# Eight matmuls of an attention kernel's opening moved into the projection, and a PSUM copy cut into two quarters

## The chip, the cores and the metric

The kernel runs on one core of a Trainium2 chip. The metric is the device time of one execution in microseconds (us). A run lists two numbers: its **time**, and its **span**, which is the time from the first to the last instruction in the records of that execution. The time is longer than the span, and I call the difference the time outside the span.

## The reference

```python
# B, Sq, D = 8, 32, 1024; Hq, Hkv, Sk, Dh = 32, 4, 8192, 128; all bfloat16
W = 2048                                    # the last W of the cache are used
q = (x @ wq).reshape(B, Sq, Hq, Dh).transpose(0, 2, 1, 3)
k = jnp.repeat(k_cache[:, :, Sk - W:, :], 8, axis=1)
v = jnp.repeat(v_cache[:, :, Sk - W:, :], 8, axis=1)
p = softmax(einsum("bhqd,bhkd->bhqk", q, k) * Dh ** -0.5)
o = einsum("bhqk,bhkd->bhqd", p, v)
return o.transpose(0, 2, 1, 3).reshape(B, Sq, Hq * Dh) @ wo
```

## The kernel before

There are 32 units (8 batches by 4 KV heads). A unit is four steps; each step multiplies four K tiles with the queries of eight heads (scores), takes the exponential on ScalarE, and multiplies the result with V two steps later. TensorE does the multiplications, and also the Q projection, the output projection, and the turning (transposing) of some K tiles. Its results lie in PSUM, from where VectorE or ScalarE copies them. The 256 rows of x are two row tiles of 128, and wq, the weight matrix of the Q projection, arrives in 8 chunks of 128 rows; the "late" matmuls make the second row tile of heads 4 to 7, which the first scores don't need. The opening, which the change edits, must make Q of the first KV head and a transposed K0 before the first scores:

```python
self.ps_m = pool("ps_m", 2, long_ctx, space=PSUM)
self.ps_s = pool("ps_s", 2, space=PSUM)       # scores, and in the opening K0's transposes
...
def start(self):
    ...
    wq0 = self.load_wq(0, 0, (1, 1, 1, 1)) + self.load_wq(0, 1, (2, 1, 1))  # chunks 0..3, then 4+5, 6, 7
    ...                                       # then K0, V0, K1, ... on the same queue
    x_turn(0, self.ps_m, "m"); x_turn(1, self.ps_s, "s_ps")
    ...
    for c in range(self.DC):                  # 8 chunks of D
        for h in range(self.rep):             # 8 heads: 4 with both row tiles, 4 with the first only
            q_mm(c, h)
        ...
    tp = [self.ps_s.tile([P, KT, P], BF16, name="kf_ps", tag="s_ps") for _ in range(2)]
    k_turn(0)                                 # 8 transposes: K0's first half
    q_copy(...)                               # Q of batch 0, out of PSUM (ScalarE, VectorE)
    k_copy(0)                                 # VectorE: the whole first half, 128x1024
    self.late = self.q_late(4, 2)             # second row tiles of heads 4 and 5
    self.late[0]()                            # head 4: 8 "late" matmuls
    k_turn(1)                                 # 8 transposes: K0's second half
    k_copy(1)
    self.va_copy(0)
    ...

# run(), every step:
    s_ps = self.ps_s.tile([P, CJ, UQ], FP32, name="s_ps")
    for jj in range(CJ):
        nc.tensor.matmul(s_ps[:, jj, :], lhsT=self.kT[ui][:, c * CJ + jj, :], rhs=q_u, start=True, stop=True)
```

The first scores take the buffer that held K0's first half, so they may only be written when that half has been copied out entirely.

## Time and profile before

| | before |
|---|---|
| time, median of 3 runs | 183.78 us (183.70 to 184.23) |
| span of the profiled run | 182.3 us |
| first transposes of x (x has landed) | 4.50 us |
| first transposes of K0 | 11.29 us |
| first scores | 12.69 us |
| start of the last long group of matmuls | 175.49 us |

The lines that the prediction reads (busy shares, the chain of waits, what TensorE's weight loads, PEld in the profile, stop for, VectorE's copies) are shown there. Two marks serve in all that follows. **S** is the start of the first scores in the timeline of TensorE. **E** is the start of the last group of 34 output matmuls in the chain of waits. Between S and E TensorE has the same instructions in both kernels:

```profile
12.69 0.61 PE L505 MATMUL s_ps<-QT,kT 128*128 128x256 bf16 x4
```

```profile
30.34 0.60 PE s_ps L505 x4
...
175.49 3.94 PE op_ps L322 x34
```

The first fence is a line of TensorE's timeline (start, duration, instruction), the second two of the chain of waits. E - S is 175.49 - 12.69 = 162.80 us.

### The profile page before, as it was taken

What the parts mean: (1) busy time and instruction counts of PE and PEld (TensorE: products, weight loads), DVE (VectorE), ACT (ScalarE), POOL (GpSimd) and SP (SyncE); (2) the same over time, 40 slices, a digit from 0 to 9 for tenths busy, and PEclk for the clock granted to TensorE, in tenths of its full rate; (3) what the DMA queues carried; (4) which work ended last, traced back from release to release, by engine and by line L of the source; (5) the groups of instructions that cost most, each with busy time, mean ns of one, the idle gap of its engine ahead of it and who ended that gap; (6) DMA issues with size and microseconds to landing.
All of it is one profiled execution on the core that took longest, in us unless ns stands there. A gap on an engine that the chain in (4) does not pass through costs nothing.

```text
span 182.3 us, 5017 instructions
## 1 busy us (share of the span) xinstructions
PE 177.4 (97%) x2026; PEld 152.0 (83%) x2041; DVE 126.0 (69%) x257; ACT 136.2 (75%) x147; POOL 89.2 (49%) x138
## 2 busy tenths in 40 slices
PE   7999999999999999999999999999999999999993
PEld 2899998998999999988787899988787788888853
DVE  0237799769887698487799565967587987554253
ACT  2228898896897888997878787887878788888800
POOL 2003564088770895936939707929606949600000
PEclk9999999999999999999999999999999999999999
DMA  6999999999999999999999999999999999980013
GB/s 169 395 400 408 225 388 350 233 296 260 377 391 244 322 257 365 374 295 313 304 378 377 391 269 271 369 245 365 258 318 273 331 289 344 218 167 0 0 41 85
DMA packets 52954, 51.73 MB, mean 284 GB/s; under 512 B 39744, under 2 KB 40256, under 8 KB 52928
## 3 DMA queue, kind: packets, MB, share of 16 engines
q1 hardware_dynamic: 52352, 50.90, 99.3%
q10 hardware_dynamic: 576, 0.49, 0.8%
q8 instruction: 16, 0.26, 0.6%
q14 instruction: 10, 0.08, 0.1%
HBM read 41.42 MB, written 0.52 MB: 230 GB/s over the span
## 4 chain that ended last, share of the span: by engine, by line
PE 91%; DMA 6%; SPq 1%; issue 1%; DVE 0%
PE o_ps L516 30%; PE s_ps L505 30%; PE op_ps L322 14%; PE q_ps L285 10%; DMA kT<-in_k_cache_dram 4%; PE q_ps L403 3%; DMA x_sb<-in_x_dram 2%; PE ql_ps L301 1%; PE tp L244 1%; SPq L208 1%; PE xT_ps L381 1%; PE kf_ps L395 0%; SPq L200 0%; DVE o_t L332 0%; PE cnt_ps L571 0%
## 5 line engine op out<-in xcount | busy, mean ns | idle before, releaser
L507 ACT ACTIVATE pT<-s_ps 128x1024 bf16<-128x1024 f32 x128 | 128.3, 1027 | 27.7 <-PE s_ps L505 27.4
L270 POOL TENSOR_SCALAR kTv<-kb 32x512 bf16<-32x512 bf16 x126 | 84.3, 669 | 51.3 <-DVE kb L259 32.1
L516 PE MATMUL o_ps<-va,pT 128*128 128x129 bf16 x1024 | 78.8, 220 | 0.1
L516 PEld LDWEIGHTS <-pT 128*128 128x128 bf16 x1024 | 68.5, 98 | 3.1
L505 PE MATMUL s_ps<-QT,kT 128*128 128x256 bf16 x336 | 50.4, 273 | 0.2
L505 PEld LDWEIGHTS <-kT 128*128 128x128 bf16 x336 | 31.7, 98 | 9.8 <-DMA kT<-in_k_cache_dram 0.4
L322 PE MATMUL op_ps<-wo_sb,OT 128*128 128x512 bf16 (+2 forms) x129 | 32.8, 353 | 0.6
L259 DVE STREAM_TRANSPOSE kb<-k_raw 128x512 bf16<-128x512 bf16 x44 | 29.7, 691 | 1.6 <-DMA k_raw<-in_k_cache_dram 1.2
L285 PE MATMUL q_ps<-xT,wq_sb 128*128 128x256 bf16 x192 | 28.3, 273 | 0.0
L438 DVE COPY va<-v_sb 128x2048 bf16<-128x2048 bf16 x30 | 25.4, 847 | 2.0 <-DMA v_sb<-in_v_cache_dram 1.6
L505 PE MATMUL s_ps<-QT,kTv 128*128 128x256 bf16 x176 | 26.4, 273 | 0.2
L268 DVE COPY kTv<-kb 32x512 bf16<-32x512 bf16 x50 | 23.1, 462 | 1.2
L444 DVE RECIPROCAL RL_all<-o_ps 128x2 f32<-128x2 f32 x32 | 5.3, 165 | 26.3 <-PE o_ps L516 26.1
L505 PEld LDWEIGHTS <-kTv 128*128 128x128 bf16 x176 | 16.9, 98 | 6.5 <-issue 0.4
L285 PEld LDWEIGHTS <-wq_sb 128*128 128x128 bf16 x192 | 16.9, 98 | 1.2
L450 DVE STREAM_TRANSPOSE OT<-o_sb 128x256 bf16<-128x256 bf16 x32 | 14.3, 445 | 1.1
L448 DVE TENSOR_TENSOR o_sb<-o_ps,RL_all 128x256 bf16<-128x256 f32 x32 | 13.6, 424 | 1.1
L322 PEld LDWEIGHTS <-OT 128*128 128x128 bf16 x144 | 11.4, 98 | 2.3 <-DVE OT L450 0.2
L436 POOL TENSOR_SCALAR va<-v_sb 128x2048 bf16<-128x2048 bf16 x2 | 3.8, 1897 | 17.0 <-DMA v_sb<-in_v_cache_dram 17.0
L288 ACT CAST QT<-q_ps 128x512 bf16<-128x512 f32 x12 | 7.0, 583 | 0.2 <-PE q_ps L285 0.2
L329 DVE TENSOR_TENSOR oacc<-op_ps,oacc 128x512 f32<-128x512 f32 x8 | 5.3, 662 | 2.0 <-PE op_ps L322 2.0
L332 DVE TENSOR_TENSOR o_t<-op_ps,oacc 128x512 bf16<-128x512 f32 (+2 forms) x6 | 3.1, 514 | 3.8 <-remote 2.2
(35 smaller groups left out, 45.0 us busy)
## 6 DMA issues: line engine op xcount, KB each, us to landing
v_sb<-in_v_cache_dram SPq DMA_DIRECT2D x30, 512.0 KB, 6.6
wo_sb<-in_wo_dram SPq DMA_DIRECT2D x16, 512.0 KB, 6.4
wq_sb<-in_wq_dram SPq DMA_DIRECT2D x13, 512.0 KB, 6.6
k_raw<-in_k_cache_dram SPq DMA_DIRECT2D x13, 512.0 KB, 5.7
wq_sb<-in_wq_dram SPq DMA_DIRECT2D x6, 256.0 KB, 4.5
v_sb<-in_v_cache_dram SPq DMA_DIRECT2D x4, 256.0 KB, 5.2
kT<-in_k_cache_dram SPq DMA_TRANSPOSE x36, 7.1
k_raw<-in_k_cache_dram SPq DMA_DIRECT2D x2, 256.0 KB, 5.7
```

The lines of the kernel that those rows point to most:

```text
L259: nc.vector.transpose(out=st["kb"][:, sl, :], in_=self.k_raw[ui][:, sl, :])
L268: nc.vector.tensor_copy(out=out, in_=in_)
L270: nc.gpsimd.tensor_scalar(out=out, in0=in_, scalar1=1.0, scalar2=1.0, op0=ALU.mult, op1=ALU.mult)
L285: nc.tensor.matmul(st[k][:, hl % 2, :], lhsT=self.wq_t[g, i][:, c % (DC // 2), hl * P:(hl + 1) * P], rhs=self.xT[:, c, :], start=(c == 0 a ...
L288: nc.scalar.copy(out=self.q_view(g)[:, :, 2 * k:2 * k + 2, :].rearrange("p b h s -> p h b s"), in_=st[k][:, :, :].rearrange("p h (b s) -> ...
L322: nc.tensor.matmul(ps[:, 0:w], lhsT=self.OT[:, gq, c, t * P:(t + 1) * P], rhs=self.wo_t[gq][:, c, n0:n0 + w], start=(k == 0), stop=(k == 7))
L438: self.nc.vector.tensor_copy(out=out, in_=in_)
L448: nc.vector.tensor_tensor(out=o_sb[:, :, :, :], in0=o_ps[:, :, 0:Dh].rearrange("p q (i c) -> p q c i", c=4), in1=rl[:, ui * QT_N:(ui + 1) ...
L450: nc.vector.transpose(out=self.OT[:, g * QT_N:(g + 1) * QT_N, :, b * self.Sq:(b + 1) * self.Sq], in_=o_sb[:, :, :, :])
L505: nc.tensor.matmul(s_ps[:, jj, :], lhsT=self.kT[ui][:, c * CJ + jj, :], rhs=q_u, start=True, stop=True)
L507: nc.scalar.activation(out=pT[:, :, :], in_=s_ps[:, :, :], func=ACT.Exp, bias=0.0, scale=self.scale)
L516: nc.tensor.matmul(o_ps[:, qt, 0:self.VW], lhsT=pT[:, jj, qt * P:(qt + 1) * P], rhs=va[:, j, 0:self.VW], start=(j == 0 and qt == 0), stop= ...
```

## The change

It means to give TensorE something to do where it stops for a chunk of wq, by putting head 4's late matmuls between the chunks, and to get the first K tiles out of PSUM sooner, by copying the first half in two quarters. The core of the diff:

```diff
-    def q_late(self, h0, n):
+    def q_late(self, h0, n, st=None):
...
-        def piece(i):
-            if i == 0:
+        def piece(i, cs=None):
+            if "ps" not in st:
                 st["ps"] = self.ps_m.tile([P, n, P], FP32, name="ql_ps", tag="m")
-            for c in range(DC):
+            for c in range(DC) if cs is None else cs:
...
-        def k_copy(half):
-            sl = slice(half * KT // 2, (half + 1) * KT // 2)
-            nc.vector.tensor_copy(out=self.kT[0][:, sl, :], in_=tp[half][:, 0:KT // 2, :])
+        def k_copy(copy, j0, j1):
+            copy(out=self.kT[0][:, j0:j1, :], in_=tp[2 * j0 // KT][:, j0 % (KT // 2):j0 % (KT // 2) + j1 - j0, :])
...
+        self.late = self.q_late(4, 2)
         for c in range(self.DC):
             for h in range(self.rep):
                 q_mm(c, h)
+            self.late[0](cs=(c,))
...
+        k_copy(nc.vector.tensor_copy, 0, KT // 4)
+        k_copy(nc.vector.tensor_copy, KT // 4, KT // 2)
         q_copy(nc.scalar.copy, 4, 8, 1, self.B // 2)
-        k_copy(0)
-        self.late = self.q_late(4, 2)
-        self.late[0]()
         k_turn(1)
-        k_copy(1)
+        k_copy(nc.vector.tensor_copy, KT // 2, KT)
```

More of the change, by code (lines that the diff above doesn't have):

```diff
@@ L291, in q_pieces @@
         return [lambda h=h, i=i: piece(h, i) for h0 in range(0, self.rep, n) for i in range(2) for h in range(h0, h0 + n)]
-    def q_late(self, h0, n):
+    def q_late(self, h0, n, st=None):
         nc, P, DC, B = self.nc, self.P, self.DC, self.B
-        st = {}
-        def piece(i):
-            if i == 0:
+        st = {} if st is None else st
+        def piece(i, cs=None):
+            if "ps" not in st:
                 st["ps"] = self.ps_m.tile([P, n, P], FP32, name="ql_ps", tag="m")
-            for c in range(DC):
+            for c in range(DC) if cs is None else cs:
                 nc.tensor.matmul(st["ps"][:, i, :], lhsT=self.wq_t[0, c // (DC // 2)][:, c % (DC // 2), (h0 + i) * P:(h0 + i + 1) * P],
@@ L306, in piece @@
                      in_=st["ps"][:, :, :].rearrange("p h (b s) -> p h b s", b=B // 2))
-        return [lambda i=i: piece(i) for i in range(n)]
+        return [lambda i=i, **kw: piece(i, **kw) for i in range(n)]
     def o_pieces(self, g, t, cuts=(512, 512), st=None):
```

## The prediction

> **What bounds the kernel now.** I read the page first, for the busy shares and for the chain of waits that ended last:
>
> ```profile
> PE 177.4 (97%) x2026; PEld 152.0 (83%) x2041; DVE 126.0 (69%) x257; ACT 136.2 (75%) x147; POOL 89.2 (49%) x138
> PE 91%; DMA 6%; SPq 1%; issue 1%; DVE 0%
> ```
>
> TensorE is the chain: 91% of the span, and no other engine has a lasting part in it. The 6% of DMA are two stretches, the load of x at the start and one transposing K load in the middle. So the next view was what TensorE's weight loads ever stop for (columns: engine, line, releaser, us in total, times, longest). I leave out the warm-up, which comes before any data:
>
> ```profile
> PEld L505 <- DMA kT<-in_k_cache_dram: 0.4, 1, 0.4
> PEld L505 <- issue: 0.4, 1, 0.4
> ...
> PEld L403 <- DMA wq_sb<-in_wq_dram: 0.2, 1, 0.2
> ```
>
> Three short stops between 5 and 170 us, all before 44 us. Their places decide this case. The timeline of weight loads puts the last of the three at 8.64 us (0.16 us, for a chunk of wq), the "issue" one at 30.31 us (the first K tile turned by VectorE and GpSimd, unit 4), and the DMA one at 43.46 us (second half of unit 6's K). Third view: the chain in order of time (start, us, what), through the part the change edits and around the last stop:
>
> ```profile
> 5.85 5.61 PE q_ps L403 x64
> 11.46 0.45 PE kf_ps L395 x8
> 11.90 0.45 PE ql_ps L301 x8
> 12.35 0.45 PE kf_ps L395 x8
> 12.80 0.50 PE s_ps L505 x4
> ...
> 34.05 0.45 PE s_ps L505 x4
> 34.50 0.66 SPq L200
> ...
> 36.74 6.67 DMA kT<-in_k_cache_dram
> 43.42 0.05 issue
> 43.46 0.61 PE s_ps L505 x4
> ```
>
> The second to fifth lines are the opening: eight transposes of K0's first half, the eight late matmuls of head 4, eight transposes of the second half, the first scores. The chain times an instruction by its end; the timeline gives starts of 11.29, 11.74, 12.19 and 12.69 us for the same four groups. The last fence shows that the path changes hands: up to 43.42 us a K transfer sets it, and only from there does TensorE run to the end without a stop.
>
> I don't believe the link at 34.05, from a score matmul to the issue of a K load. In the built program the loads issued from 10 to 37 us wait for TensorE only where it had passed long ago (the latest such count is unit 0's last scores, done at about 16.4 us); otherwise each waits for the load eight issues before it. A wait for several semaphores is easily put down to the wrong one. So 43.42 is a date of the DMA stream, and does not move when TensorE moves by tenths.
>
> The timeline of VectorE has the copies concerned (start, us, instruction):
>
> ```profile
> 11.94 0.69 DVE L399 COPY kT<-kf_ps 128x1024 bf16<-128x1024 bf16 x1 [0.45 <-PE kf_ps L395]
> 12.84 0.69 DVE L399 COPY kT<-kf_ps 128x1024 bf16<-128x1024 bf16 x1 [0.20 <-PE kf_ps L395]
> 13.44 0.68 DVE L438 COPY va<-v_sb 128x2048 bf16<-128x2048 bf16 x1
> ```
>
> A copy starts 0.65 us after the first of its eight transposes starts (11.29 to 11.94, 12.19 to 12.84), and a next copy may start about 0.09 us before the last one ends (13.53 against 13.44). The first scores start at 12.69, just after the first copy ends (11.94 + 0.69 = 12.63): the eight late matmuls filled that wait exactly.
>
> **What the Trainium skill says.** "TensorE: Matmul & The Clock Gate", section "Wait — 56ns, not 53.3ns?", gives 55.6 ns between matmuls with 128 columns; the trace has eight in 0.45 us, 56 ns, so it agrees. "VectorE: DVE Perf Modes", section "The TRN2 errata", has 120 cycles plus the elements over the mode's factor for a copy out of PSUM: at 0.96 GHz and a factor of two, 392 ns for 512 elements and 658 for 1024. The trace has 424 ns (the copy of xT, 128x512 bf16) and 691 ns: some 32 ns more, but the same slope, and a fixed part of about 157 ns which a split pays twice. I use the trace. "PSUM — Partial Sum Buffer", section "PSUM bank collisions raise a hardware error", asks for guarding by bank and quadrant, not by address. Half of K0 is 8 x 128 bf16 = 2 KiB a partition, which is one whole bank of those in that page, so neither a quarter's copy beside the other quarter's transposes nor a score write beside the second quarter's copy would be allowed. No run here shows a collision, but the waits in the program are laid out accordingly. "Perfetto Trace Analysis", section "What 'DMA-bound' means", names an issuing sequencer that is solid with DMA work as a bound of its own. The trace agrees in that SyncE's issues follow one another nearly without gaps from 17 to 43 us (single issues of 3.12, 4.67, 3.09 us).
>
> **The change part by part.** No instruction of TensorE is added or removed; eight matmuls move. VectorE gets one copy more.
>
> 1. The eight late matmuls (0.45 us) move into the projection, one after each chunk. The first needs a PSUM buffer whose last reader is ScalarE's copy of xT, over at about 6.42 us; it comes at 5.85 + 4 x 0.109 + 4 x 0.056 = 6.51, so no stop. By the fifth chunk four of them (0.22 us) have run, which is more than the 0.16 us stop for wq: it goes. The projection with its late matmuls ends 0.45 - 0.16 = 0.29 us later, so the transposes of K0 start at about 11.29 + 0.29 = 11.58 us.
> 2. The sixteen transposes now run on end: 11.58 to 12.48 us. In the old order TensorE reached this point at 12.64, so 0.16 us are gained to here.
> 3. The copies. In the built program the first quarter's copy waits for the count of the eighth transpose, not of the fourth, and the second has no wait of its own. So the first starts at 11.58 + 0.65 = 12.23; the second at 12.23 + 0.42 - 0.09 = 12.56, and it ends at 12.98.
> 4. The first scores' weight load waits for the count of both quarters. It has to: their PSUM buffer is the one both are copied from. So they start at 12.98 + 0.06 = 13.04 instead of 12.69: 0.35 us later. The gain of 0.16 becomes an idle stretch of 13.04 - 12.48 = 0.56 us, since the late matmuls that lay beside the copy are gone. The split itself costs 0.76 - 0.69 = 0.07 of it.
> 5. The second scores wait for the third copy, which starts at 12.98 - 0.09 = 12.89 and ends at 13.58. They come after four scores (0.44 us) and eight late matmuls (0.45 us), at 13.93: no stop. VectorE's later copies of the opening move by 0.05 us, so nothing waits for them that didn't.
> 6. So TensorE is 0.35 us behind from 13 us on. At 30.08 us it used to reach unit 4 and stood until 30.34, for VectorE's moves of K that ended at 30.20. That sequence starts at 19.23 us, when its K data land, and VectorE is then busy nearly throughout, so it doesn't move. TensorE now comes at 30.43: 0.26 of 0.35 us are absorbed, 0.09 stay.
> 7. At unit 6 TensorE used to be free at 42.73 + 0.44 = 43.17 and stood until 43.46, for the K data of 43.42. It now comes at 43.26 and starts at 43.46 as before. Nothing is left.
>
> The sum at the end is 0.35 - 0.26 - 0.09 = 0, against a median of 183.78 us. The opening has 0.55 us of slack (0.26 + 0.29) behind it, and the change moves it inside that slack. I add 0.05 us for what the slack may fail to take: 183.85 us.
>
> **The rivals.**
> - The opening's gain reaches the end. For it: 0.16 us of a stop goes, and the chain of waits runs through the opening. Against it: the wait for both quarters, and the two later stops, which would grow by any gain. It would make 183.6 us.
> - The loss reaches the end. For it: the chain draws the K load of 43.42 as released by TensorE at 34.05; if that is right, or if the moves of unit 4 follow TensorE, 0.09 to 0.35 us stay. Against it: the counts that the loads wait for. It would make 183.9 to 184.15 us.
> - The DMA stream shifts by itself. A landing at 19.23 or 43.42 that comes 0.3 us sooner or later moves the end by up to as much, in either kernel. The three runs before spread over 0.53 us, as much as all that is at stake.
> - A hidden wait, such as K0's second half landing later than the sixteen transposes now want it (at about 12.0 instead of 12.13 us). It would add tenths in the opening at most, and the slack takes them.
>
> **Range and chances.** The rivals span 183.6 to 184.15; runs differ by 0.3 us from the median and more. So 183.85, with 183.45 to 184.25 for 8 in 10. 2% are 3.7 us, ten times the largest single term, so within 2% is all but certain; a slower or faster state would be needed for anything else: 0.01 each.
>
> **What would show it.** Steps 1 and 2: no wait for wq in the projection, sixteen transposes on end from about 11.6 us. Steps 3 and 4: two copies of 0.42 us from about 12.2 us, the first scores at about 13.0, with TensorE's weight loads idle for some 0.5 us and VectorE's copy as releaser. Steps 6 and 7: the "issue" stop at unit 4 shrunk to nearly nothing, the first scores of unit 6's second half still at about 43.45, for the DMA. Wrong would be first scores before 12.7 us (then the quarters do overlap the transposes), or a landing at 43.42 that moves with TensorE, or a difference above 0.5 us.

## The result, and the profile after

| | before | changed |
|---|---|---|
| time, median | 183.74 us (183.55 to 184.23, 4 runs) | 184.80 us (184.65 to 185.08, 4 runs) |
| ratio of times | 1 | 1.0055 (95%: 1.0032 to 1.0079) |
| span of the profiled run | 182.3 us | 182.2 us |
| time less span, profiled run | 1.75 us | 2.88 us |

A ratio is the mean time of one kernel's fast runs over that of the other's in the same rounds, so it isn't quite the ratio of the medians. 184.80 us lies outside the predicted range of 183.45 to 184.25, and all four runs of the changed kernel are above it.

The profile after, page first (busy time by engine, chain by engine):

```profile
PE 177.9 (98%) x2041; PEld 152.2 (84%) x2041; DVE 125.5 (69%) x258; ACT 136.2 (75%) x147; POOL 89.1 (49%) x138
PE 93%; DMA 3%; SPq 1%; DVE 1%; issue 0%
```

VectorE has one instruction more. TensorE's 177.9 us against 177.4 is no change of work: the trace of before lacks 15 of 144 records of the output projection, hence 2026 matmuls against 2041 weight loads. In the chain, DVE has come in and DMA has halved. What weight loads stop for between 5 and 170 us (engine, line, releaser, us in total, times, longest):

```profile
PEld L402 <- DMA wq_sb<-in_wq_dram: 0.6, 1, 0.6
PEld L505 <- DVE kT L398: 0.6, 1, 0.6
```

Before, there were three stops, of 0.16 us in the projection, 0.36 us at unit 4 and 0.41 us at unit 6. Now there are two, both in the opening, and the two later ones are gone. (The weight load of K0's second transposes, for one, starts at 12.13 us and its matmuls at 12.19. So the two later stops cost the matmuls less than the whole 0.77 us: 0.57, by the comparison of E - S below.) The timeline shows where (weight loads, then TensorE's transposes, VectorE's copies, the first scores):

```profile
8.99 0.66 PEld L402 LDWEIGHTS <-wq_sb 128*128 128x128 bf16 x8 [0.60 <-DMA wq_sb<-in_wq_dram]
...
11.87 1.06 PE L395 MATMUL kf_ps<-ident,k_raw 128*128 128x128 bf16 x16
...
12.51 1.35 DVE L398 COPY kT<-kf_ps 128x512 bf16<-128x512 bf16 x3 [0.50 <-PE kf_ps L395]
...
13.33 0.61 PE L505 MATMUL s_ps<-QT,kT 128*128 128x256 bf16 x4 [0.41 <-DVE kT L398]
```

The first line is a stop of 0.60 us for the fifth chunk of wq, which the prediction held to be gone. The second: sixteen transposes on end. The third: three copies, no two of them apart, which start when the eighth transpose is done. The fourth: the first scores at 13.33 us, held up by the copies; before, they started at 12.69. The chain of the same run:

```profile
12.03 0.46 PE kf_ps L395 x8
...
12.51 0.77 DVE kT L398 x2
...
13.33 0.61 PE s_ps L505 x4
...
43.70 0.44 PE s_ps L505 x4
...
175.56 3.94 PE op_ps L322 x34
```

The chain goes through two copies on VectorE, where it used to stay on TensorE. At 43.70 us nothing is waited for: the K data which set the pace in the trace of before had come in time. E - S is 175.56 - 13.33 = 162.23 us, 0.57 less than before. So in this pair of traces the opening is 0.64 us longer, 0.57 of it is gained back by stops that no longer happen, and the ends are only 0.07 us apart. Taken alone that looks like the predicted slack at work. But the times differ by 1.0 us, so the pair leaves two questions: do those later stops belong to the kernel before at all, and where is the rest?

### The profile page after: what moved, and what is told of

It is laid out like the page before. It is cut to its first block, busy times and chain, and to the rows that moved or that the text cites. A ratio compares the mean times of both kernels' runs of the same rounds, so it can differ in the third digit from the quotient of the medians.

```text
span 182.2 us, 5032 instructions
## 1 busy us (share of the span) xinstructions
PE 177.9 (98%) x2041; PEld 152.2 (84%) x2041; DVE 125.5 (69%) x258; ACT 136.2 (75%) x147; POOL 89.1 (49%) x138
## 4 chain that ended last, share of the span: by engine, by line
PE 93%; DMA 3%; SPq 1%; DVE 1%; issue 0%
PE o_ps L516 32%; PE s_ps L505 31%; PE op_ps L322 15%; PE q_ps L285 12%; DMA wq_sb<-in_wq_dram 3%; PE q_ps L402 2%; PE tp L244 1%; SPq L168 1%; PE ql_ps L301 1%; DVE kT L398 0%; PE kf_ps L395 0%; SPq L347 0%; DVE o_t L332 0%; PE cnt_ps L571 0%
## 5 line engine op out<-in xcount | busy, mean ns | idle before, releaser
L322 PE MATMUL op_ps<-wo_sb,OT 128*128 128x512 bf16 (+2 forms) x144 | 36.0, 355 | 0.0
L268 DVE COPY kTv<-kb 32x512 bf16<-32x512 bf16 x50 | 22.6, 452 | 1.2
L402 PE MATMUL q_ps<-xT,wq_sb 128*128 128x256 bf16 (+1 forms) x64 | 5.9, 246 | 0.4 <-DMA wq_sb<-in_wq_dram 0.4
```

The source lines that it names most:

```text
L268: nc.vector.tensor_copy(out=out, in_=in_)
L322: nc.tensor.matmul(ps[:, 0:w], lhsT=self.OT[:, gq, c, t * P:(t + 1) * P], rhs=self.wo_t[gq][:, c, n0:n0 + w], start=(k == 0), stop=(k == 7))
L402: nc.tensor.matmul(ps, lhsT=self.wq_t[0, c // H][:, c % H, h * P:(h + 1) * P], rhs=self.xT[:, c, 0:n], start=(c == 0 and h in (0, 2, 4)), ...
```

## The experiments

Twelve runs were made, all with correct results, in three calls, each on a chip of its own with 11 runs of the kernel before beside it. Every kernel has 6 runs. The expectations name my theories by letters. In words: the extra microsecond lies outside the span (A) or inside it (B), as the first two expectations say; the loss of the opening reaches the end one for one, because the later stops of before were an accident of one trace (C); or a slack of about 0.55 us absorbs it, as predicted (D); the rest of the blind difference is brought about by the moved matmuls and lies outside the span (E); or it is no property of the program (F).

Median times and mean spans of the kernel before were 184.06 and 182.16 us in the first call, 183.85 and 181.99 in the second, 184.12 and 182.16 in the third.

### The kernel before, again

```diff
+# the kernel before, unchanged
```

> The kernel before once more, with a comment line added, under the same measuring as the others. It gives what the result lacked: several times of the old kernel, each with the span of its own trace. Theory A (the extra microsecond lies outside the traced span): time 183.7 us, ratio 1.000, spans near 182.2 us, so time minus span about 1.5 us, against 2.1 to 2.9 us in the four runs of the changed kernel. Theory B (the extra microsecond lies inside the span, and the profile of before was an unlucky long one): spans of the null kernel near 181.3 us, and time minus span as in the changed kernel, about 2.5 us.

Measured: 183.68 us, ratio 0.9977 (0.9936 to 1.0019), mean span 181.78 us. The chain of waits in its trace:

```profile
12.88 0.50 PE s_ps L506 x4
...
30.32 0.44 PE s_ps L506 x4
...
43.15 0.44 PE s_ps L506 x4
...
175.00 3.94 PE op_ps L323 x34
```

From 14 to 170 us no weight load stops for anything. The first scores of unit 4 and the second half of unit 6 run straight on, in 0.44 us each, without the wait for VectorE's moves or for K data. S is 12.77 us in the timeline, E - S is 162.23 us. The same program as before thus has E 0.49 us earlier, and no stop behind its opening. Neither A (spans near 182.2 us) nor B (near 181.3) is met as a whole: the mean span lies between, and 1.96 us lie outside it.

### The changed kernel, again

```diff
+# the changed kernel, unchanged
```

> The changed kernel once more. If the 1.0055 is a property of the program, it comes again: 184.7 us, ratio 1.004 to 1.007. If it was the chip or the hour, the ratio is within 1.002 of 1. Theory A: spans 182.0 to 182.6 us as before; theory B: the same spans, but about 1 us above those of the null kernel.

Measured: 184.19 us, ratio 1.0007 (0.9968 to 1.0046), mean span 182.20 us. Its only stop from 5 to 170 us:

```profile
PEld L506 <- DVE kT L399: 0.6, 1, 0.6
```

Here the stop for wq is indeed gone, as predicted; the one for the copies has stayed. S is 12.94, E 175.17, E - S again 162.23 us. The blind difference of 0.55% did not come again.

### The late matmuls alone

The changed kernel, with K0's first half copied in one piece:

```diff
-        k_copy(nc.vector.tensor_copy, 0, KT // 4)
-        k_copy(nc.vector.tensor_copy, KT // 4, KT // 2)
+        k_copy(nc.vector.tensor_copy, 0, KT // 2)
```

> The changed kernel with the first half of K0 copied in one piece again; so only the moved late matmuls (and the order of two copies on different engines) remain. My prediction's working makes its first scores 0.07 us sooner than in the changed kernel, nothing at the end. Theory A or B with the moved matmuls as the cause: 184.7 us, ratio 1.005. With the split as the cause: ratio 1.000.

Measured: 184.74 us, ratio 1.0028 (0.9988 to 1.0069), mean span 182.25 us. Timeline:

```profile
11.83 1.06 PE L395 MATMUL kf_ps<-ident,k_raw 128*128 128x128 bf16 x16
13.22 0.61 PE L504 MATMUL s_ps<-QT,kT 128*128 128x256 bf16 x4 [0.34 <-DVE kT L398]
...
12.47 1.29 DVE L398 COPY kT<-kf_ps 128x1024 bf16<-128x1024 bf16 x2 [0.50 <-PE kf_ps L395]
```

From the first transpose to the first scores it takes 13.22 - 11.83 = 1.39 us, the same as before (1.40): the copy sets this distance, with or without matmuls beside it. What the move does is to take eight matmuls out from beside the copy, where they cost nothing, and put them into the projection ahead of it. That is the loss in this kernel, which has no quarters. The time itself can't tell: its interval holds both expected ratios, 1.000 and 1.005.

### The quarters alone

The kernel before, with the first half copied in two:

```diff
-        k_copy(0)
+        k_copy(nc.vector.tensor_copy, 0, KT // 4)
+        k_copy(nc.vector.tensor_copy, KT // 4, KT // 2)
```

> The kernel before with the first half of K0 copied in two quarters, the late matmuls where they were. My working: the first scores 0.07 us later than before, nothing at the end. If the split (one instruction of VectorE more, and a copy of two) causes the loss: ratio 1.005. If the moved matmuls cause it: ratio 1.000.

Measured: 184.05 us, ratio 0.9996 (0.9949 to 1.0042), mean span 182.20 us. Timeline:

```profile
11.93 0.61 PE L395 MATMUL kf_ps<-ident,k_raw 128*128 128x128 bf16 x8
...
13.39 0.61 PE L505 MATMUL s_ps<-QT,kT 128*128 128x256 bf16 x4
```

1.46 us from first transpose to first scores, against 1.40: the quarters cost 0.06 us in the opening and gain nothing, since the scores wait for both. (The interval of the times again holds both 1.000 and 1.005.) In the changed kernel the same distance is 13.33 - 11.87 = 1.46 us. This trace also had stops of 0.3 and 0.7 us for wq in a projection that the edit does not touch.

### Chunks 4 and 5 of wq as two loads

The kernel before, and then the changed kernel, with a finer load, meant to take the stop for wq away:

```diff
-        wq0 = self.load_wq(0, 0, (1, 1, 1, 1)) + self.load_wq(0, 1, (2, 1, 1))
+        wq0 = self.load_wq(0, 0, (1, 1, 1, 1)) + self.load_wq(0, 1, (1, 1, 1, 1))
```

> The kernel before, with the second half of wq's first group loaded in four pieces of 256 KB instead of one of 512 and two of 256. In the six traces so far TensorE waited 0 to 1.0 us for wq in the projection, mostly for that 512 KB piece. Theory C (what happens in the opening reaches the end one for one, as first scores and last output matmuls were 162.23 us apart in five of six traces): the wait goes, first scores at about 12.5 us, span 0.2 to 0.4 us shorter than before, ratio 0.998 to 0.999. Theory D (my prediction's: the opening has half a microsecond of slack behind it): no difference at the end, 1.000.

> The same for the changed kernel. With no wait left to fill, the moved late matmuls cost their full 0.45 us and the split 0.07. Theory C: first scores about 0.5 us later than in e5_before_wq4, and the last output matmuls too; time 0.5 us above it, ratio to before about 1.001. Theory D: the end is where it is in e5_before_wq4.

Measured: 184.57 us, ratio 1.0028 (1.0005 to 1.0050), mean span 182.53 us; and with the change 185.05 us, 1.0059 (1.0034 to 1.0084), mean span 182.80 us. Both expectations missed: the time rose, and the first scores came at 13.27 and 13.04 us, not at 12.5 and half a microsecond later. The timeline of the first:

```profile
10.50 1.53 PE L403 MATMUL q_ps<-xT,wq_sb 128*128 128x256 bf16 x16 [0.51 <-DMA wq_sb<-in_wq_dram]
```

The stop moved from the fifth chunk to the seventh and grew; its weight load stood for 0.68 us. One load more stands in the queue ahead of the last chunks and ahead of K0. In the second trace there is no stop for wq, but weight loads stand for 0.17 us in the opening for K0's second half, and for 0.31 and 0.68 us later for K data and their moves, so its E - S is 163.03 us. I take the longer queue for the cause of both without having tested that. The changed kernel has the longer mean span here too, by 0.27 us, but in the two traces its first scores come earlier, so this pair does not show that the opening makes the difference.

### The first quarter in a PSUM tile of its own

The change's two aims, without the wait for the second quarter: the first quarter gets one tile, the other three share the other; a Q copy goes to ScalarE and head 6's late matmuls come one step sooner, so that VectorE is free.

```diff
+        def slot(j0, j1):
+            at = 0 if j0 < KT // 4 else KT // 4
+            return tp[1 if at else 0][:, j0 - at:j1 - at, :]
...
+        k_copy(nc.vector.tensor_copy, 0, KT // 4)
+        q_copy(nc.scalar.copy, 0, 2, 1, self.B)
         k_turn(1)
+        k_copy(nc.vector.tensor_copy, KT // 4, KT // 2)
+        k_copy(nc.vector.tensor_copy, KT // 2, KT)
...
-Q_LATE = {6: 1, 7: 9}
+Q_LATE = {6: 0, 7: 9}
```

> The changed kernel with the wait undone that made its split useless: the first quarter of K0 is transposed into a PSUM tile of its own, so its copy waits for four transposes only, and the first scores for that copy alone. (The other three quarters go to the other tile; one copy of q moves to ScalarE and head 6's late matmuls come one slot sooner, so that nothing else waits.) From the measured durations: first scores 0.91 us after the first transpose instead of 1.46, so 0.55 us sooner than in the changed kernel at equal arrival of data. Theory C: the last output matmuls then come about 0.5 us sooner too, 0 to 0.2 us before those of the kernel before; ratio 0.999. Theory D: no difference at the end.

> Both: quarter in its own tile and four pieces of wq. With nothing left to wait for, theory C: first scores at about 12.4 us, the end within 0.1 us of e5_before_wq4, ratio 0.998. Theory D: 1.000.

Measured: 184.34 us, ratio 1.0020 (0.9999 to 1.0040), mean span 182.07 us; with the finer load of wq 184.40 us, 1.0031 (1.0012 to 1.0051), mean span 182.70 us. Timeline of the first:

```profile
11.79 1.06 PE L399 MATMUL kf_ps<-ident,k_raw 128*128 128x128 bf16 x16
12.70 0.61 PE L509 MATMUL s_ps<-QT,kT 128*128 128x256 bf16 x4
...
12.22 0.42 DVE L402 COPY kT<-kf_ps 128x512 bf16<-128x512 bf16 x1 [0.28 <-PE kf_ps L399]
```

The first copy now starts with only the first four transposes behind it, beside the rest of them, and the first scores start 0.91 us after the first transpose instead of 1.46, straight after the sixteenth. The stop for the copies is gone: this is the wait that the change failed to take away. The gain gives back what the moved matmuls and the quarters had cost, so its spans are at the level of the kernel before (182.07 against 181.99 us) and no better. Little was to be won beyond that, for before has no idle time in its opening other than the stop for wq, and this trace stood at unit 4 as that of before did (0.20 us). The expected ratio of 0.999 was missed: in the mean the time is 0.33 us longer than before, of which 0.08 is span. With the finer load the first scores came at 13.37 us instead of the expected 12.4. No kernel beats the one before.

### A delay of known size

The kernel before, with K0's first eight transposes done five times over: 32 matmuls of 56 ns more, 1.79 us, ahead of everything that was to have slack.

```diff
-        k_turn(0)
+        for _ in range(5):
+            k_turn(0)
```

> The kernel before with the eight transposes of K0's first half done five times (same result): 32 useless matmuls, 1.79 us, put into the opening on purpose. Theory C (one for one): first scores and last output matmuls stay 162.23 us apart unless K data are late; spans and times 1.8 us above those of before, ratio 1.0097. Theory D (half a microsecond of slack behind the opening in the usual execution): 1.25 us, ratio 1.0068.

Measured: 185.51 us, ratio 1.0089 (1.0035 to 1.0142), with one run of 187.82. The interval of the times holds both theories. The spans tell them apart better: their median is 183.7 us against 182.0 of the kernel before, so 1.7 of 1.79 us arrive at the end, where a slack of 0.55 would have let 1.24 through. (Six runs are few: resampling them and the 11 beside them, that is drawing them at random with repeats, puts this difference at 1.3 to 3.0 us in 95% of the draws. A slack of 0.55 in every execution is unlikely by that, one in some executions is not excluded.) And the trace (timeline, then chain):

```profile
14.88 0.61 PE L506 MATMUL s_ps<-QT,kT 128*128 128x256 bf16 x4
```

```profile
177.11 3.94 PE op_ps L322 x34
```

E - S = 177.11 - 14.88 = 162.23 us, the same to the hundredth as in the first repeat of the undelayed kernel. Against that trace nothing was absorbed; but that one has no stop behind its opening that could absorb anything, so the reason has to be read elsewhere. VectorE's last moves for unit 4, the date of the prediction's step 6, show it (before, first repeat, delayed kernel; then a copy of the delayed kernel that stands ahead of the moves):

```profile
26.94 3.25 DVE L268 COPY kTv<-kb 32x512 bf16<-32x512 bf16 x6
26.68 3.25 DVE L269 COPY kTv<-kb 32x512 bf16<-32x512 bf16 x6
28.78 3.25 DVE L268 COPY kTv<-kb 32x512 bf16<-32x512 bf16 x6
```

```profile
22.65 0.69 DVE L246 COPY kT<-tp 128x1024 bf16<-128x1024 bf16 x1 [0.23 <-PE tp L244]
```

From S to the end of these moves it takes 17.50, 17.16 and 17.15 us. So with the delay the moves came 2.10 us later than in the first repeat, as the first scores did (2.11): the date follows TensorE. VectorE's work ahead of the moves waits for TensorE, as in the last line for K tiles that TensorE turned.

### Three kernels again, on a third chip

The late matmuls alone, the changed kernel, and the kernel before, without further edits, to see whether the time outside the span goes with the program.

```diff
+# three kernels as above, unchanged
```

> e3_late_only again, on whatever chip comes, for what lies between the measured time and the traced span. There it was 1.8 us in 1 of 6 executions and 2.3 to 2.9 in 5, against 1.7 to 1.9 in 8 of 11 of the kernel before. Theory E (the moved matmuls cause it, by whatever way): again more than half of the executions above 2.2 us. Theory F (it comes and goes with any program): 1 to 3 of 6 above 2.2 us. The span, by theory C, about 0.3 us above before.

> The changed kernel a third time, for the size of its loss. So far 1.0055 on the first chip and 1.0007 on the second. Theory C with F: span 0.2 to 0.5 us above before, ratio 1.001 to 1.003. Theory E: 1.004 to 1.006, with more than half of the executions more than 2.2 us outside the span.

> The kernel before with a comment, for how far two equal programs lie apart in one job: it was 0.9977 the first time. Expected within 0.998 to 1.002, with 1 to 3 of 6 executions more than 2.2 us outside the span by theory F, none or one by theory E.

Measured: 184.30 us, ratio 1.0009 (0.9968 to 1.0050); 184.06 us, 0.9986 (0.9948 to 1.0023); 183.81 us, 0.9973 (0.9935 to 1.0011). Mean spans: 182.17, 182.20, 181.95 us. A copy of the kernel before lies 0.23% and 0.27% below its own original in two calls, so that much is noise. Measured against these copies, the changed kernel is 1.0007 / 0.9977 = 1.0030 and 0.9986 / 0.9973 = 1.0013, that is 0.55 and 0.24 us slower; against the 11 runs of before beside it, it is 0.07% slower and 0.14% faster. Each ratio is known to about 0.4%, so no time of these two calls shows the loss. The trace of the late matmuls alone does, for it has no stop for wq:

```profile
5.87 0.82 PE L402 MATMUL q_ps<-xT,wq_sb 128*128 128x256 bf16 x8
...
12.99 0.61 PE L504 MATMUL s_ps<-QT,kT 128*128 128x256 bf16 x4 [0.34 <-DVE kT L398]
```

From the first matmul of the projection to the first scores it takes 7.12 us, and 7.18 in the changed kernel (second and third trace); before, it was 6.84 (first and third call's trace), with a stop for wq of 0.16 us in it. So of the 0.34 us that the change loses there, the moved matmuls make 0.28 and the quarters 0.06.

### What the runs give together

| trace | x landed | stop for wq | S | E | E - S |
|---|---|---|---|---|---|
| before | 4.50 | 0.16 | 12.69 | 175.49 | 162.80 |
| before, again | 4.36 | 0.4 | 12.77 | 175.00 | 162.23 |
| before, third call | 4.33 | 0.2 | 12.52 | 174.89 | 162.37 |
| changed | 4.19 | 0.6 | 13.33 | 175.56 | 162.23 |
| changed, again | 4.38 | none | 12.94 | 175.17 | 162.23 |
| changed, third call | 4.41 | none | 12.99 | 175.22 | 162.23 |

(us; "x landed" is the start of x's transposes.) In ten of all fourteen traces E - S is 162.22 to 162.24 us, with S anywhere from 12.77 to 14.88; in the same ten VectorE's last moves for unit 4 end 17.14 to 17.16 us after S. In the other four they end 17.27 to 17.50 us after S, and 10.96 to 10.99 us after VectorE's first work on their K data, for which it had stood idle 0.94 to 1.19 us (in the ten at most 0.75). These are the changed kernel with the finer load (E - S 163.03) and the three traces with S at 12.70 or earlier: the two of before with 162.80 and 162.37, and the own tile (162.35). So the end of the moves follows the later of two dates, that of the data and that of the opening, and only where the data set it can the stop at unit 4 take up part of a loss. The stop at unit 6 stands in the trace that I predicted from and in no other.

| | runs | mean span | time less span: mean | of these runs, above 2.2 us |
|---|---|---|---|---|
| kernel before, all runs with a span from the three calls | 45 | 182.04 | 1.98 | 9 |
| changed, blind result | 4 | 182.30 | 2.53 | 3 |
| changed, two later calls | 12 | 182.20 | 1.96 | 1 |
| late matmuls alone, two calls | 12 | 182.21 | 2.32 | 8 |

The time outside the span is mostly 1.7 to 2.1 us, and in some executions of most programs 2.2 to 3.1, without a sharp border. Three of the four blind runs of the changed kernel are above 2.2, but only one of its next twelve, with the same instructions on the same queue: 4 of 16, against 9 of 45 before, so these counts show no effect of the change. The late matmuls alone have 8 of 12 there, which by itself would speak for the moved matmuls, yet the changed kernel moves the same ones. What puts an execution above 2.2 us is open. The chip of the blind pair wasn't measured again, so its part in it is open too.

## Why the prediction was wrong

**Steps 1 and 2** (the projection and the transposes) were right in mechanism. The late matmuls come without a stop of their own, and the sixteen transposes run on end in every trace of the changed kernel. "More than the 0.16 us stop for wq: it goes" was a figure of one trace: the stop measures 0.16 to 0.4 us in three traces of before, 1.0 us in all with the quarters alone, and in the changed kernel none, none and 0.6. Four late matmuls, at 56 ns each, can fill 0.22 us of it, no more.

**Steps 3 and 4** (the copies and the first scores) were right. The copies take 0.42, 0.42 and 0.69 us with 0.09 of overlap at each joint, 1.35 in all. The scores wait for both quarters, the stop is 0.57 us against 0.56 predicted, and the quarters' own part is 0.06 against 0.07. Counted from x's landing, S comes at 8.56 and 8.58 us in the two traces of the changed kernel without a stop for wq, and at 8.19, 8.41 and 8.19 in those of before, on average 0.31 us later against the 0.35 predicted. In the blind trace it is 9.14, for its stop of 0.6.

**Step 5** was right: the second scores wait for nothing.

**Steps 6 and 7 failed**: "The opening has 0.55 us of slack (0.26 + 0.29) behind it, and the change moves it inside that slack." What failed is "so it doesn't move" in step 6, and the date of 43.42 us in step 7, taken as fixed. In the trace I read, K data happened to come late, and set both dates. In ten of fourteen traces they did not: there the moves of unit 4 follow the first scores at 17.15 us, and TensorE finds no stop to shrink. In the other two traces of the kernel before, the two stops together are none and 0.14 us (162.37 - 162.23). The prediction's term of 0.26 + 0.09 us absorbed would thus be 0.35, 0 and 0.14 us in the three traces of before, and my estimate from these is that 0.19 us of the loss of 0.35 reach the end on average. The spans fit that: 182.20 less 182.04 us is 0.16 us of mean span in the later calls (0.0 to 0.3 by resampling the runs), 0.26 for the blind runs' 182.30, 0.3 by the medians of all spans (182.2 against 181.9), and a delay put in on purpose came through with 1.7 of 1.79 us. I had this as the second rival, with 183.9 to 184.15 us, and had named its condition: that the moves of unit 4 follow TensorE. The median of all 16 runs of the changed kernel, 184.20, lies 0.3 us above that of 45 of the kernel before, 183.87.

**The range** failed for another reason. With the whole loss of 0.35 us at the end, the forecast would have been about 184.1 us, still inside the range. I put the spread of runs at 0.3 us and more from the median, from three runs of one call. The blind difference of means is 184.83 - 183.82 = 1.01 us. Against the 45 runs of before, 0.26 us of that is span, 2.53 - 1.98 = 0.55 is time outside the span, and 0.2 is that the four runs of before beside it were faster than its average (183.82 against 184.03). Only the first has a cause that the traces show, and its size is known no better than said above; the 0.55 us are not explained. I had not looked at the time outside the span at all, although the trace of before and its time (182.3 and 184.05 us) showed that it exists.

The first rival (the gain of the opening reaches the end) fell, since there was no gain. The third, the DMA stream shifting by itself, is what made the slack look like a property of the program. The fourth, K0's second half coming too late for the sixteen transposes, showed only with the finer load of wq, as 0.17 and 0.18 us in the changed kernel and in that with its own tile.

## What to carry to other kernels

Eight matmuls beside a copy cost nothing here (1.40 us from transposes to scores with them, 1.39 without), and moving them elsewhere left the wait bare, so look for what stands in the gap before you empty it; cutting a copy helps only if its consumer may start on the first part, which here the shared PSUM buffer forbids until the first part has a tile of its own. A stop late in one trace isn't slack until a second trace of the same program has it too, and until you know whether the date that it waits for stands still or follows the work you move: mark two instants with the same work between them and compare their distance over several executions. For changes of tenths of a us, compare spans as well as times, and know how far the time outside the span wanders before setting a range.

## What the Trainium skill lacked or had wrong

- "VectorE: DVE Perf Modes", section "The TRN2 errata", gives by its formula 392 and 658 ns for copies of 512 and 1024 bf16 elements out of PSUM (120 cycles plus half the elements). The runs show 0.42 and 0.69 us for these copies of K0: the slope is right, the fixed part about 32 ns short. By that formula alone a split would cost 0.125 us (an estimate: the fixed part once more); with the overlap of 0.09 us between two copies it measured 0.06.
- No page that I read tells how far the arrival of the same load moves between executions of one program. Here the stop for a chunk of wq in an unchanged projection was 0.16 to 1.0 us, and the stops for K data and its moves in the kernel before cost 0 to 0.57 us.
- "Runtime: NRT & Kernel Launch" treats what surrounds a kernel's own instructions, but I found nothing there on how far it varies between executions of one program. Here the time less the span was 1.8 to 3.1 us for one program on one chip (the kernel before, third call), which is a wider spread than the change itself.
